# Gated attention, then a gated long convolution: the last batch's gate projections are put at the end of the planner's order, and the first loads are reordered

## The chip, the cores and the metric

The kernel runs on one core of one Trainium2 chip. Its time is the device time of the whole program in microseconds (us), the median of several runs. A profile of one execution shows what each engine did: PE is TensorE (PEld its weight loads), DVE is VectorE, ACT is ScalarE, POOL is GpSimd, SP is the engine that here only issues DMAs.

## The reference

For each of 8 batches, with u and v of 3136 x 256 and z of 3136 x 64:

```
attn = relu(z z^T / S)^2              # S = 3136
x    = u * (attn v)                   # 3136 x 256
x1, x2, x3 = split(x @ w_proj)        # three times 3136 x 256
conv = irfft(rfft(x2) * rfft(filter)) # circular convolution over the sequence
out  = (x1 * conv * x3) @ w_out
```

## The kernel before, in words

The sequence is cut into 25 tiles of 128 rows (the last holds 64) and into seven chunks of 512, 384, 512, 384, 512, 384 and 448 columns. For each batch and chunk the kernel makes score tiles (`score_mm`, L1334), takes their relu on ScalarE (L1509), squares them on ScalarE or VectorE (L1516, L1518) and multiplies them with v into two accumulators (`weigh`, L1364). Part of the squared tiles are turned by a transposing DMA and used again for a later chunk (L1449). The chunk's result times u is `xT` (L1558), the transposed x.

From `xT`, `add_proj` makes two things. `to_gates` computes x1 (L896), copies it out of PSUM, computes x3 (L908) and multiplies the two into a gate tile (L916), for each half of the 256 columns: 14 gates a batch. `to_spectrum` computes x2 (L939), puts it through the first stage of a Fourier transform (L756) and writes it to DRAM. When all seven chunks of a batch are written, `add_spectrum` loads them in another order (L788), does the second stage (L809, L817), multiplies with the filter's spectrum (L1011), goes back (L809, L825) and writes to DRAM again (L1061). `add_end` loads that (L800), does the last stage (L1100, L1097), multiplies with the gates into `yT` (L1103), multiplies with w_out (L1131) and stores the output (L1159).

None of this is issued in the order of the code. The steps are tasks of a planner (`Plan`), which runs when the kernel is built: it keeps a model of each engine's time, takes for each engine the task that can start first, and so writes out each engine's instruction order, which the chip then follows strictly. For TensorE there are five queues: S (scores), W (attention times v), FA (projections and first transform stage), FB (spectrum and outputs) and FZ. In each of the last three the first six tasks are looked at, in S and W only the first one. A queue comes into play when its task can start now; FZ is always the last of the list:

```
order += ["FA", "FB", "W", "FZ"] if self.credit > 0 else ["W", "FA", "FB", "FZ"]
```

For the other engines a task's `prio` decides among those that can start at the same time; a lower number goes first. A `Pool` of n buffers is in the planner a row of n slots: a task that takes a slot waits until an earlier one is free. `ps_m` is the pool of two PSUM banks through which projections, spectrum and outputs go; once no W task is left, the planner also lends them the other banks.

Around the end: the gates are FA tasks. Batch 6 stores three of its seven output chunks during batch 7 (FB); the other four are FZ tasks that wait for the last square of batch 7, and their stores wait until the last spectrum load of batch 7 is issued. The seven output chunks of batch 7 are FB tasks, with buffers borrowed from pools that are no longer used. An output chunk's last transform stage waits for all 14 gates of its batch.

At the start, before the planner: ten DMAs load z of batch 0 (L451), seven issued by SP and three by ScalarE; POOL issues the loads of v and u (L418, L399) in the order v tiles 0 to 6, u chunk 0, v tiles 7 to 13, u chunk 1, w_proj (L473), v tiles 14 to 24. `V_AT` and `U_AT` are the times at which the planner takes v (first part, rest) and u (chunk 0, chunk 1) as there. The table `T1` of the first transform stage is a sine (L636) of angles that VectorE makes.

## Time and profile before

| | us |
|---|---|
| median of 3 runs (lowest, highest) | 1051.87 (1051.53, 1052.62) |
| the profiled execution, whole | 1055.78 |
| its span, first to last instruction | 1053.9 |

| engine | busy us | share of the span | instructions |
|---|---|---|---|
| PE | 1003.5 | 95% | 6078 |
| DVE | 819.7 | 78% | 1485 |
| ACT | 914.6 | 87% | 1285 |
| POOL | 185.2 | 18% | 401 |

The mean granted clock of TensorE is 0.981 of full speed. The DMAs moved 167.99 MB, 159 GB/s over the span. Matmuls are pipelined and their ends are modelled, so 95% for PE is not 95% of its peak. A busy share over the whole span mixes stages with different limits: the start, eight batches, and a tail after the last attention matmul. The chain of work that ended last is followed back from the last instruction, at each step to what released it.

### The profile page before, as it was taken

The page shows a single profiled execution, that of the slowest core. Times are in us where ns is not written, and L with a number is a line of the kernel's source. Part 1 is how long each engine was busy: PE and PEld are TensorE (multiplying, and loading weights), DVE is VectorE, ACT ScalarE, POOL GpSimd, SP SyncE. Part 2 cuts the span into 40 slices and gives each one's busy share as a digit, 9 for nine tenths or more (in the row PEclk, how much of TensorE's full clock was granted, in tenths as well). Part 3 has the DMA queues.
Part 4 walks back from the last instruction along what each step waited for, and adds up shares of the span by engine and source line. Part 5 has one row for each costly group of instructions (what it writes and reads, how often), then busy time and mean ns, then how long its engine had stood idle before and what let it go on. Part 6 is the DMA issues. An engine that isn't in the chain of part 4 may idle for free.

```text
span 1053.9 us, 17942 instructions
## 1 busy us (share of the span) xinstructions
PE 1003.5 (95%) x6078; PEld 487.5 (46%) x6078; DVE 819.7 (78%) x1485; ACT 914.6 (87%) x1285; POOL 185.2 (18%) x401
## 2 busy tenths in 40 slices
PE   5999899999999999999999999999999999999874
PEld 2443434444444444445444454445454454444553
DVE  6767479968798688887889777986889877997653
ACT  6998799979899699998899899997999989997642
POOL 5123111211022201222022210212021210010000
PEclk9999999999999999999999999999999999999966
DMA  9699857888878878898979888888888888666447
GB/s 155 108 165 176 157 114 140 158 153 191 174 152 132 160 178 183 162 150 185 183 134 170 158 192 188 148 151 145 185 177 167 157 170 188 127 133 151 109 149 203
DMA packets 324380, 167.99 MB, mean 159 GB/s; under 512 B 234088, under 2 KB 302184, under 8 KB 324288
## 3 DMA queue, kind: packets, MB, share of 16 engines
q1 hardware_dynamic: 296320, 135.69, 60.0%
q0 software_dynamic: 27728, 30.97, 21.4%
q8 instruction: 48, 0.79, 0.3%
q14 instruction: 44, 0.36, 0.1%
q10 hardware_dynamic: 240, 0.18, 0.1%
HBM read 90.26 MB, written 53.35 MB: 136 GB/s over the span
## 4 chain that ended last, share of the span: by engine, by line
PE 75%; DVE 7%; DMA 7%; ACT 6%; issue 3%; SPq 2%; ACTq 0%; DVEq 0%; POOL 0%; POOLq 0%
PE ps_o_t L1364 38%; PE ps_s_t L1334 11%; PE ps_m_t L908 4%; PE ps_m_t L939 4%; PE ps_m_t L896 3%; PE ps_m_t L1131 3%; ACT R_t L1509 3%; PE ps_m_t L756 2%; DMA M_t<-A_t 2%; DVE xT_t L1558 2%; PE ps_m_t L817 2%; DVE A_t L1518 2%; PE ps_m_t L1100 2%; PE ps_m_t L825 2%; DVE xh L1011 2%
## 5 line engine op out<-in xcount | busy, mean ns | idle before, releaser
L1509 ACT ACTIVATE R_t<-ps_s_t 128x1024 f32<-128x1024 f32 (+2 forms) x552 | 485.6, 917 | 30.4 <-PE ps_s_t L1334 23.2
L1364 PE MATMUL ps_o_t<-A_t,v_t 128*128 128x512 bf16 (+2 forms) x2064 | 471.1, 354 | 1.8 <-DVE A_t L1518 1.5
L1364 PEld LDWEIGHTS <-v_t 128*128 128x128 bf16 x2688 | 253.0, 98 | 239.7 <-issue 33.4
L1518 DVE TENSOR_TENSOR A_t<-R_t 128x1024 bf16<-128x1024 f32 (+3 forms) x286 | 305.5, 1075 | 44.0 <-ACT R_t L1509 33.0
L1516 ACT ACTIVATE A_t<-R_t 128x1024 bf16<-128x1024 f32 (+4 forms) x266 | 251.2, 953 | 11.9 <-DMA M2e_t<-A_t 3.0
L1334 PE MATMUL ps_s_t<-zT_t 64*128 64x512 bf16 (+2 forms) x1088 | 155.1, 357 | 3.4 <-ACT R_t L1509 2.7
L408 POOL COPY tick<-xT_t 1x1 bf16<-1x1 bf16 x54 | 10.1, 188 | 748.4 <-DVE xT_t L1558 748.4
L916 DVE TENSOR_TENSOR gate_t<-ps_m_t,x_t 128x256 bf16<-128x256 f32 (+1 forms) x222 | 72.8, 382 | 40.5 <-PE ps_m_t L908 28.8
L1558 DVE SCALAR_TENSOR_TENSOR xT_t<-ps_o_t,uT_t 128x256 bf16<-128x256 f32 (+1 forms) x224 | 76.2, 381 | 30.8 <-PE ps_o_t L1364 17.0
L359 ACT ACTIVATE x_t<-ps_m_t 128x512 bf16<-128x512 f32 (+3 forms) x131 | 70.0, 557 | 25.1 <-PE ps_m_t L896 15.6
L1011 DVE TENSOR_TENSOR xh<-xh,H 100x1024 bf16<-100x1024 bf16 x120 | 81.6, 683 | 6.2 <-ACT xh L359 5.3
L1334 PEld LDWEIGHTS <-zT_t 64*128 64x128 bf16 x1088 | 33.2, 94 | 101.6 <-issue 97.8
L1364 PE MATMUL ps_o_t<-M_t,v_t 128*128 128x384 bf16 (+2 forms) x336 | 79.1, 345 | 1.1 <-DMA M_t<-A_t 1.1
L1103 DVE TENSOR_TENSOR yT_t<-ps_m_t,gate_t 128x512 bf16<-128x512 f32 (+2 forms) x98 | 59.3, 621 | 22.3 <-PE ps_m_t L1100 18.6
L363 DVE CAST x_t<-ps_m_t 128x512 bf16<-128x512 f32 (+3 forms) x90 | 54.9, 625 | 14.1 <-PE ps_m_t L939 8.0
L399 POOL DMA_DIRECT2D un_t<-in_u_dram x112 | 60.0, 558 | 6.9 <-issue 5.5
L418 POOL DMA_DIRECT2D v_t<-in_v_dram x112 | 59.7, 555 | 5.4 <-issue 2.4
L896 PE MATMUL ps_m_t<-xT_t,wp 128*128 128x512 bf16 (+2 forms) x222 | 56.1, 353 | 3.5 <-DVE xT_t L1558 3.0
L939 PE MATMUL ps_m_t<-wp,xT_t 128*128 128x256 bf16 x392 | 57.3, 274 | 0.0
L908 PE MATMUL ps_m_t<-xT_t,wp 128*128 128x512 bf16 (+2 forms) x222 | 54.8, 354 | 0.3 <-ACT x_t L359 0.2
L363 DVE CAST s_t<-ps_m_t 128x512 bf16<-128x512 f32 (+1 forms) x67 | 42.3, 640 | 15.0 <-PE ps_m_t L756 14.4
L359 ACT ACTIVATE xh<-ps_m_t 100x512 bf16<-100x512 f32 (+1 forms) x89 | 52.5, 612 | 0.6 <-PE ps_m_t L1131 0.4
(179 smaller groups left out, 965.5 us busy)
## 6 DMA issues: line engine op xcount, KB each, us to landing
out_dram<-ost_t SPq DMA_DIRECT2D x49, 256.0 KB
spec<-s_t SPq DMA_DIRECT2D x88, 128.0 KB
spec_in_t<-spec SPq DMA_DIRECT2D x28, 392.0 KB
spec<-gs_t SPq DMA_DIRECT2D x28, 392.0 KB
out_dram<-ost_t SPq DMA_DIRECT2D x47, 192.0 KB
v_t<-in_v_dram POOLq DMA_DIRECT2D x56, 128.0 KB, 4.3
un_t<-in_u_dram POOLq DMA_DIRECT2D x56, 128.0 KB, 5.1
conv_in_t<-spec SPq DMA_DIRECT2D x26, 256.0 KB
```

The costliest lines, as they stand in the source:

```text
L359: nc.scalar.activation(out_, in_, AF.Copy)
L363: nc.vector.tensor_copy(out_, in_)
L896: nc.tensor.matmul(box["p"][:, :cw], wp16[:, k, ds(nb * P, P)], xt["t"][:, k, :cw], start=(k == 0), stop=(k == 1),)
L908: nc.tensor.matmul(box["p3"][:, :cw], wp16[:, k, ds((4 + nb) * P, P)], xt["t"][:, k, :cw], start=(k == 0), stop=(k == 1),)
L939: nc.tensor.matmul(box["p"][:, ds(k_ * D, D)], xt["t"][:, k, ds((at + k_) * P, P)], wp16[:, k, ds(D, D)], start=(k == 0), stop=(k == 1),)
L1011: nc.vector.tensor_tensor(x[:, 1 - i], x[:, 0], h, ALU.mult)
L1334: nc.tensor.matmul(ps[:m, i, :cw], zt[h, ds(t * P, m)], zt[h, ds(C0[c], cw)], start=True, stop=True)
L1364: nc.tensor.matmul(o, row(v16[b], t)[:, ds(dh * P, P)], x, start=(k == 0 and i == 0), stop=(last and i == len(pair) - 1),)
L1509: nc.scalar.activation(box["R"][:rows, 0:n, :cw], live[un][:rows, 0:n, :cw], AF.Relu)
L1516: nc.scalar.activation(a, r, AF.Square)
L1518: nc.vector.tensor_tensor(a, r, r, ALU.mult)
L1558: nc.vector.scalar_tensor_tensor(x, f, inv_s2, ut, ALU.mult, ALU.mult)
```

## The change

The gate tasks of the last batch go to FZ instead of FA, and their two evictions get prio 2 instead of 0. The pool of x buffers has eight instead of two. An output chunk waits for its own gate alone, not for all of the batch. At the start SP issues all ten loads of z, and POOL issues v whole, then u chunks 0 and 1, then w_proj. The planner's times for v and u are set anew, and it takes the sine's first step as possible from 6.6 us.

```diff
-    xT_p = Pool("xT", 2, [P, 2, 512], BF16)
+    xT_p = Pool("xT", 8, [P, 2, 512], BF16)
...
-            q = nc.scalar if j == 0 and t0 == ZF else nc.sync
-            q.dma_start(
+            nc.sync.dma_start(
                 out=zf[lo // ZF][...], in_=zr[...]
             )
...
     load_rows(v16[0], v[0], 0, 7)
     u_nat = {}
-    cast_u(0, 0)
...
     load_rows(v16[0], v[0], 7, 14)
+    load_rows(v16[0], v[0], 14, NT)
+    cast_u(0, 0)
     cast_u(0, 1)
     wp16 = const.tile([P, 2, 3 * D], BF16, name="wp16")
     nc.gpsimd.dma_start(out=wp16[:], in_=moe_w_proj.rearrange("(t p) n -> p t n", p=P))
-    load_rows(v16[0], v[0], 14, NT)
...
-    ZF_AT, V_AT, U_AT = (4.5, 6.0, 7.0), (9.0, 16.0), (13.0, 18.0)
+    ZF_AT, V_AT, U_AT = (4.5, 6.0, 7.0), (8.0, 15.0), (19.0, 22.0)
...
-    def sin_steps(box, w, first, dst=None):
+    def sin_steps(box, w, first, dst=None, at=0.0):
...
-        ta = step("DVE", a, c_dve(w), takes=[gs_p.slots])
+        ta = step("DVE", a, c_dve(w), takes=[gs_p.slots], at=at)
...
-    t1_done, _ = sin_steps({}, P, t1_first, T1[:, :])
+    t1_done, _ = sin_steps({}, P, t1_first, T1[:, :], 6.6)
...
+        kind, late = ("FZ", 2) if b == B - 1 else ("FA", 0)
...
-                a = pe("FA", mm1, c_pe(cw, cw), xt_tasks, [ps_m.slots, x1_p.slots])
-                e1 = job(None, ev1, both(cw), [a])
+                a = pe(kind, mm1, c_pe(cw, cw), xt_tasks, [ps_m.slots, x1_p.slots])
+                e1 = job(None, ev1, both(cw), [a], prio=late)
                 e1.frees.append((a, 0))
-                a3 = pe("FA", mm3, c_pe(cw, cw), [*xt_tasks, a], [ps_m.slots, g_p.slots])
-                e3 = on("DVE", ev3, c_dve(cw), [a3, e1])
+                a3 = pe(kind, mm3, c_pe(cw, cw), [*xt_tasks, a], [ps_m.slots, g_p.slots])
+                e3 = on("DVE", ev3, c_dve(cw), [a3, e1], prio=late)
...
                 a = pe(
-                    kind, mm, c_pe(*[P] * nt), [ld, t4_done, *firsts, *(e for _, e in gtasks), *then],
+                    kind, mm, c_pe(*[P] * nt), [ld, t4_done, *firsts, gtasks[2 * c + dh][1], *then],
```

## The prediction

> **What bounds the kernel now.** I read four things in this order: the page's chain that ended last, the chain in order of time over the last batch, the busy table by stage, and the order of time at the head. One profiled execution took 1055.78 us with a span of 1053.9 us, so 1.9 us lie around the span; the median of the three runs is 1051.87, which is 3.9 lower. I sum against the profiled execution and carry the difference over to the median unchanged.

> The page's shares by engine:

> ```profile
> PE 75%; DVE 7%; DMA 7%; ACT 6%; issue 3%; SPq 2%; ACTq 0%; DVEq 0%; POOL 0%; POOLq 0%
> ```

> The same chain from 886.4 us to the last attention matmul of the last batch (batch 7) at 989.64, start and length of a piece in us; the gate projections are L896 and L908:

> ```profile
> 893.04 1.00 PE ps_m_t L896 x4
> 894.04 0.33 PE ps_o_t L1364 x2
> 894.36 0.43 PE ps_s_t L1334 x4
> 894.79 0.16 PE ps_o_t L1471 x2
> 894.96 0.97 PE ps_m_t L908 x4
> 895.93 0.97 PE ps_o_t L1364 x6
> ...
> 976.35 0.65 PE ps_m_t L896 x4
> ```

> One piece begins where the one before ends: TensorE is fed without a gap, so a matmul that leaves this stretch shortens it by its own length. The busy table by stage (length; busy us of PE, PEld, DVE, ACT, POOL; granted clock; DMA share; GB/s):

> ```profile
> 886.40:989.64 103.24, 102.95 (x622) 49.59 (x622) 83.41 (x151) 89.45 (x128) 6.92 (x16) 1.00 0.65 142
> 989.64:998.27 8.63, 6.93 (x68) 4.96 (x64) 7.30 (x16) 4.95 (x10) 0.00 (x0) 1.00 0.47 132
> 998.27:1026.00 27.73, 21.99 (x95) 15.68 (x95) 14.64 (x23) 15.16 (x27) 0.00 (x0) 0.63 0.47 142
> 1026.00:1031.50 5.50, 0.00 (x0) 0.00 (x0) 0.69 (x2) 0.00 (x0) 0.00 (x0) 0.71 0.76 199
> 1031.50:1053.90 22.40, 12.88 (x100) 9.80 (x100) 8.33 (x14) 7.10 (x15) 0.00 (x0) 0.65 0.74 198
> ```

> The first row is bound by TensorE at full clock. The others are the tail, a chain of latencies: last x, spectrum out and in (8.63 us), spectrum products (27.73), second round trip (5.50, every engine idle), output. There TensorE has gaps, but its clock falls to 0.63 to 0.71.

> **Gates out of the last batch.** On the chain between 886.4 and 989.64, L908 has 5.0% and L896 4.6%: 9.6% of 103.24 us = 9.9 us. This is chunks 0 to 5, 12 gates of four matmuls each (0.22 us for 512 columns); chunk 6 comes after the attention already. If all of them leave, TensorE loses 9.9 us here. VectorE loses about 24 products of 0.42 and 0.35 us (L916), 9 us, and 12 evictions of about 0.56 us, 6.7 us, leave ScalarE or VectorE. Do these two engines follow? From 900 to 940 they are busy 76.4 of 80 us; without two chunks' gates (four, 5.2 us) it is 71.2 of 2 x 36.6, or 97%. That is too tight to be free, so I give back 1.0 us there (between 0, if TensorE stays the bound, and 3, if the two become it). Gates that the planner drops into a hole of its own schedule stay in this stretch; they cost at most what they cost now. Main stage: **-8.9 us**.

> **The same gates in the tail.** They stand first in FZ, and the planner looks at six tasks of it, so they come ahead of batch 6's last four output chunks, which share that queue and now fill 989.64 to 998.27 (8 of their products L1103 and 20 matmuls L1131). A gate takes two PSUM banks and one of two x1 buffers; its chain of four operations takes about 2 us, so two in flight give one per 1.0 us, and VectorE alone allows one per 0.76. In 8.63 us 8 to 11 of the 14 gates get done; about 4.5 gates and nearly all of batch 6's end move on into the stage from 998.27. That is 4.5 x 0.83 = 3.7 us of matmul and 26 x 0.055 + 28 x 0.108 = 4.5, less 0.9 that lies there already: 7.3 us at full clock. VectorE and ScalarE get about 14 us more and have 13.1 + 12.6 idle, so they hide it. TensorE has 27.73 - 21.99 = 5.7 us idle. At the clock of 0.5 that the two-microsecond rows show from 1002 to 1014, 7.3 becomes 14.6, and the stage grows by 8.9. The 5.5 us round trip, where all is idle, takes some of that; with it the growth is 3.4. At full clock the stage needs 21.99 x 0.63 = 13.9 + 7.3 = 21.2 us of TensorE and (14.64 + 15.16 + 14) / 2 = 22 us of the other two, so it would shrink by 3 to 5. Which? The clock falls where TensorE goes slack:

> ```profile
> 996.00:998.00 2.00, 0.72 (x5) 0.41 (x5) 1.12 (x3) 0.87 (x2) 0.00 (x0) 1.00 0.58 189
> 998.00:1000.00 2.00, 1.29 (x7) 0.87 (x8) 0.00 (x0) 1.06 (x3) 0.00 (x0) 1.00 0.03 11
> 1000.00:1002.00 2.00, 0.74 (x4) 0.45 (x4) 1.91 (x3) 1.00 (x3) 0.00 (x0) 0.74 0.63 200
> 1002.00:1004.00 2.00, 2.00 (x11) 1.91 (x10) 0.77 (x2) 0.60 (x1) 0.00 (x0) 0.50 0.00 1
> ```

> The moved gates fill just these gaps, so I expect the fall later than now but not gone: **+2.0 us**, between -5 and +9. [...]

> Batch 6's stores (1728 rows of 1 KB, 1.77 MB) wait for the last spectrum load to be issued (1015.1 now), so a later end of batch 6 costs nothing until its products come after that. The stores then run at 230 to 320 GB/s, 6 to 8 us of DMA time. I take no cost, 0 to 7 as bounds.

> **Eight x buffers.** With two, x of chunk c+2 waits for the users of c; chunks lie about 16 us apart and the users end within that, so in batches 0 to 6 nothing waits on it, and the cost is nothing (only PE ps_m_t L896 <- DVE xT_t, 0.3 us, shows on PE between 868 and 989). In batch 7 they are the cover of the move: with two, deferred gates would stop x itself. The narrower wait of the outputs for their own gate changes nothing before batch 7, as the spectrum ends after the gates.

> **The head.** ScalarE's queue at the start, from order of time:

> ```profile
> 4.78 3.77 ACTq L451 DMA_DIRECT2D ost_t<-in_z_dram  x3
> 8.60 0.31 ACT L636 ACTIVATE T<-gs_t 128x128 bf16<-128x128 f32 x1 [6.35 <-DVE percol L607]
> 8.81 0.70 ACT L359 ACTIVATE xT_t<-ost_t 128x256 bf16<-128x256 f32 x2
> ```

> Its three z loads hold ScalarE until 8.55; the sine's input was ready at 7.1, so without them it can start up to 1.5 us earlier. ScalarE is then busy 23.5 of 24 us to 35 us, so an earlier start is carried on. SP gets three more issues of 0.60, ending near 7.0 instead of 5.2, before the two spectrum-padding writes; its next job is at 10.6, so that is hidden. On POOL the rest of v (7 issues, 4.2 us, with 1.0 us of waits on v's own landing) goes ahead of u: the issue of u moves from 3.7 and 7.9 to about 13, w_proj from 10.3 to about 15. With some 6 us to land, u is there near 20 and its transposes on SP, with the mirror transposes queued behind them, shortly after; x of chunk 0 is made at 33.7, so 10 us cover it. The DMAs are full (0.9 and more) from 3 to 26 us in either order. The head gives -1.5 to 0 by itself, but a planner's order changes with it, and batch 0 has stalls (88.6 to 96.4 on a mirror transpose, 117.5 to 125.2 on the filter's load) that may shift either way: **-1.0**, bounds -4 and +3.

> Sum: -8.9 + 2.0 - 1.0 = **-7.9 us**; profiled 1047.9, median **1044.0**.

> **Rivals.** (a) The gates keep the clock up through the spectrum: the stage falls from 27.7 to 22 and no gap re-opens, -6 instead of +2, and the median is 1036. For it: the gaps in the four rows above are what precedes the fall. Against: the stage's products still make TensorE wait 1 to 2 us each.
> (b) Slower: batch 6's end is pushed past the second round trip. Place: its products and output matmuls (9 us at half clock) stand among batch 7's outputs after 1031.5, and its 1.77 MB are stored with the final 3.2 MB, where DMA is at 0.74 already (6 to 8 us). It decides once fewer than about half of the 14 gates are through by 998 and the clock is at 0.5. Price: 9 of the spectrum stage's growth, 7 for stores; -8.9 - 1.0 + 16 = +6, with part of it overlapping +2 to +5: 1054 to 1057. For it: the queue's order. Against: the idle 5.5 us and the idle shares of DVE and ACT.
> (c) The change does not do what it says: the planner finds enough holes in its own schedule of batch 7, and the gates stay between the attention matmuls. Then only the head is left: about 1051, 1049 to 1053. Against: the chain shows no holes there.

> **Numbers.** Forecast 0.54 (1038 to 1049), (a) 0.13, (b) 0.22, (c) 0.11. A measurement of this kernel tells 0.2% (2.1 us) from no change. Only (c) reaches the middle, and it splits into 0.03 faster, 0.04 same and 0.04 slower: faster 0.54 + 0.13 + 0.03 = 0.70, same 0.04, slower 0.22 + 0.04 = 0.26. The range leaves out half of (a) and the upper part of (b): 1036 to 1055.

> **What would show it.** Right: between the last batch's start and its last attention matmul L896 and L908 fall from 9.6% of the chain to under 2%, and that matmul lies 9 to 11 us earlier; after it the two lines fill TensorE, and batch 6's L1103 come later than 998 does now by the new clock. The tail, 64.3 us from that matmul to the end of the span, becomes 61 to 70 us, with the granted clock at 1.0 some microseconds longer. At the head the sine starts near 7 and the first score matmul (10.87) up to 1.5 us earlier. Wrong: the last matmul earlier by under 6 us (ScalarE and VectorE bind), the tail longer by over 9 us, or a gap on TensorE before 60 us that waits for u or v.

## The result, and the profile after

The changed kernel takes 1044.33 us (1042.60 to 1045.57, four runs) where before took 1051.70 beside it: a ratio of 0.9927, interval 0.9910 to 0.9945, so 7.4 us faster (5.8 to 9.5). A second measurement, beside the experiments, gave 1043.34 against 1051.87, ratio 0.9906 (0.9884 to 0.9928). Single runs of either kernel lie up to 5 us from their median, and the first profile of before was of such a run (1055.78); the profiled run of the change took 1042.60, below its median. The two profiles are therefore 13.2 us apart where the medians are 7.4 apart, and the stages must be compared one by one.

The chain's shares, from the page of the changed kernel, are nearly the same as before:

```profile
PE 75%; DVE 8%; ACT 7%; DMA 5%; issue 3%; SPq 1%; another core or an unknown queue 0%; ACTq 0%; DVEq 0%; POOL 0%; POOLq 0%
```

The chain in order of time in the middle of the last batch (start, length in us). The gate lines are now L897 and L909, and attention, scores and spectrum follow one another without them:

```profile
930.24 0.97 PE ps_o_t L1365 x6
931.21 0.48 PE ps_s_t L1335 x4
931.70 0.32 PE ps_m_t L755
932.02 0.22 PE ps_m_t L824
932.24 1.30 PE ps_o_t L1365 x8
...
967.88 0.22 PE ps_m_t L909
...
968.15 0.59 PE ps_m_t L897 x2
```

Only one gate (its halves near 924 and 968) and the first half of another (968) were still run there. From 875 us on, the two gate lines have 0.81 us of the chain, under 1% where they had 9.6%. The other ten gates of chunks 0 to 5, and the rest of that one, come right after the last attention matmul, which ends at 979.42 instead of 989.64. In order of time on TensorE:

```profile
982.38 0.59 PE L897 MATMUL ps_s_t<-xT_t,wp 128*128 128x512 bf16 x2
982.82 0.59 PE L909 MATMUL ps_o_t<-xT_t,wp 128*128 128x512 bf16 x2
983.25 0.59 PE L897 MATMUL ps_o_t<-xT_t,wp 128*128 128x512 bf16 x2
983.68 0.59 PE L909 MATMUL ps_m_t<-xT_t,wp 128*128 128x512 bf16 x2
```

The busy table by stage, cut at the same events as before (length; busy us and instructions of PE, PEld, DVE, ACT, POOL; granted clock; DMA share; GB/s):

```profile
870.60:979.42 108.82, 107.90 (x653) 51.69 (x660) 82.79 (x139) 100.52 (x139) 7.45 (x19) 1.00 0.72 154
979.42:989.24 9.82, 9.30 (x55) 4.99 (x54) 8.18 (x24) 6.90 (x13) 0.00 (x0) 1.00 0.23 69
989.24:1014.06 24.82, 20.57 (x148) 14.30 (x148) 20.13 (x37) 17.74 (x34) 0.00 (x0) 0.98 0.50 152
1014.06:1019.63 5.57, 0.00 (x1) 0.00 (x1) 0.00 (x0) 0.65 (x2) 0.00 (x0) 0.50 0.88 241
1019.63:1040.70 21.07, 10.71 (x100) 8.41 (x100) 8.28 (x14) 6.99 (x15) 0.00 (x0) 0.82 0.72 208
```

(The first row here begins at the last x of batch 6; before's began at 886.4.) The stage of the spectrum products has 53 more matmuls than before and is 2.9 us shorter, and the clock stands at 0.98 where it was 0.63; whether the clock is the cause is tested below with matmuls that nothing reads. The two-microsecond rows that answer to the slack of before:

```profile
987.00:989.00 2.00, 1.77 (x13) 0.87 (x11) 1.89 (x7) 1.53 (x3) 0.00 (x0) 1.00 0.55 177
989.00:991.00 2.00, 1.76 (x11) 1.22 (x12) 1.57 (x5) 1.09 (x2) 0.00 (x0) 1.00 0.07 28
991.00:993.00 2.00, 1.90 (x18) 1.13 (x17) 2.00 (x4) 1.14 (x3) 0.00 (x0) 1.00 0.51 146
993.00:995.00 2.00, 1.34 (x8) 0.79 (x7) 2.00 (x6) 0.60 (x1) 0.00 (x0) 1.00 0.15 54
```

Where TensorE had 0.72, 1.29 and 0.74 of 2 us it now has 1.3 or more, and the clock stays at 1.00. VectorE becomes the full engine (2.00 of 2 us from 991 to 995).

Beside the page, one table serves all runs below. I cut each profile at the last product of x (chunk 6) of each batch; "tail" runs from that of batch 7 to the end of the span. Clock is the mean granted clock of the span. "Fill" stands for the matmuls of the left-out gates with nothing that reads them.

| kernel | batches 0-2 | 3-6 | 7 | tail | clock |
|---|---|---|---|---|---|
| before, first profile | 383.3 | 487.9 | 119.1 | 63.5 | 0.981 |
| before, second | 389.7 | 487.5 | 119.1 | 63.4 | 0.981 |
| the change, first | 381.5 | 489.1 | 109.6 | 60.6 | 0.992 |
| the change, second | 379.4 | 488.3 | 109.5 | 61.8 | 0.990 |
| tail's part alone | 383.2 | 487.2 | 111.0 | 63.8 | 0.988 |
| head's part alone | 379.9 | 489.1 | 120.0 | 63.4 | 0.984 |
| all but the gates' move | 382.4 | 488.8 | 120.4 | 62.7 | 0.984 |
| x buffers alone | 389.7 | 487.1 | 119.1 | 65.4 | 0.975 |
| before, no gates | 381.9 | 486.9 | 109.7 | 63.6 | 0.983 |
| before, no gates, fill | 383.6 | 487.2 | 110.6 | 61.5 | 0.990 |
| the change, no gates | 380.4 | 488.8 | 109.0 | 64.3 | 0.983 |
| the change, no gates, fill | 382.8 | 488.8 | 109.6 | 61.9 | 0.988 |
| the change, HOLD 2 | 379.2 | 488.7 | 107.8 | 60.9 | 0.992 |
| the change, half the gates | 383.0 | 489.6 | 115.3 | 64.2 | 0.985 |

The first column differs by 6 us between two executions of one program, so the comparisons rest on the third and fourth columns, on the timed runs, and on the first two columns only where several profiles agree. Two of the profiles are of runs far above the median of their kernel: that of the x buffers alone (1063.66 us, 6.3 above) and the second one of before (1061.44, 8.1 above).

The tail holds two effects that the table adds up. From the first spectrum product to the last matmul ahead of the second round trip, the fourteen profiles take 29.8 us at a granted clock of 0.50 (x buffers alone), 27.5 to 28.3 at 0.63 or 0.64 (six: both of before, the head's part, all but the gates' move, and the two without gates and without fill), 26.8 at 0.75 (half the gates) and 22.7 to 26.1 at 0.91 to 1.00 (the other six). From the last x to the first spectrum product they take 7.8 to 8.0 us where all gates of batch 7 stay in FA, and 8.5 to 10.7 in all others, 9.3 and 10.2 in the two that leave gates out and put nothing in their place. So a higher clock goes with a shorter spectrum stage; the longer way ahead of it, which the kernels without gates have too, takes a part of that back.

### The profile page after: what moved, and what is told of

Read it like the earlier page. It is cut to its first block, busy times and chain, and to the rows that moved or that the text cites. A ratio compares the mean times of both kernels' runs of the same rounds, so it can differ in the third digit from the quotient of the medians.

```text
span 1040.7 us, 17903 instructions
## 1 busy us (share of the span) xinstructions
PE 989.8 (95%) x6010; PEld 480.7 (46%) x6078; DVE 819.1 (79%) x1497; ACT 912.6 (88%) x1273; POOL 190.4 (18%) x401
## 4 chain that ended last, share of the span: by engine, by line
PE 75%; DVE 8%; ACT 7%; DMA 5%; issue 3%; SPq 1%; another core or an unknown queue 0%; ACTq 0%; DVEq 0%; POOL 0%; POOLq 0%
PE ps_o_t L1365 40%; PE ps_s_t L1335 11%; PE ps_m_t L940 4%; ACT R_t L1510 4%; PE ps_m_t L1132 4%; PE ps_m_t L909 3%; PE ps_m_t L897 3%; PE ps_m_t L755 2%; DMA M_t<-A_t 2%; PE ps_m_t L824 2%; PE ps_m_t L1101 2%; PE ps_m_t L816 2%; DVE xT_t L1559 2%; DVE A_t L1519 2%; ACT A_t L1517 1%
## 5 line engine op out<-in xcount | busy, mean ns | idle before, releaser
L1365 PE MATMUL ps_o_t<-A_t,v_t 128*128 128x512 bf16 (+2 forms) x2011 | 465.4, 354 | 3.6 <-issue 0.5
L1519 DVE TENSOR_TENSOR A_t<-R_t 128x768 bf16<-128x768 f32 (+2 forms) x271 | 290.7, 1080 | 35.2 <-ACT R_t L1510 29.4
L1517 ACT ACTIVATE A_t<-R_t 128x768 bf16<-128x768 f32 (+3 forms) x281 | 265.8, 958 | 5.4 <-DMA spec<-s_t 0.9
L408 POOL COPY tick<-xT_t 1x1 bf16<-1x1 bf16 x54 | 15.9, 294 | 737.5 <-DVE xT_t L1559 737.5
L917 DVE TENSOR_TENSOR gate_t<-ps_m_t,x_t 128x256 bf16<-128x256 f32 (+1 forms) x208 | 69.0, 385 | 30.8 <-PE ps_m_t L909 15.1
L359 ACT ACTIVATE x_t<-ps_m_t 128x512 bf16<-128x512 f32 (+3 forms) x114 | 61.7, 564 | 16.7 <-PE ps_m_t L897 12.2
L363 DVE CAST x_t<-ps_m_t 128x512 bf16<-128x512 f32 (+3 forms) x99 | 60.0, 621 | 15.6 <-PE ps_m_t L940 10.8
L1132 PE MATMUL ps_m_t<-wo,yT_t 128*128 128x256 bf16 (+1 forms) x348 | 54.9, 278 | 0.2
L897 PE MATMUL ps_m_t<-xT_t,wp 128*128 128x512 bf16 (+2 forms) x203 | 51.7, 353 | 2.0 <-DVE xT_t L1559 1.7
L1365 PE MATMUL ps_o_t<-M2e_t,v_t 128*128 128x512 bf16 (+1 forms) x192 | 51.7, 370 | 0.3 <-issue 0.2
```

Source lines behind the costliest of these rows:

```text
L363: nc.vector.tensor_copy(out_, in_)
L897: nc.tensor.matmul(box["p"][:, :cw], wp16[:, k, ds(nb * P, P)], xt["t"][:, k, :cw], start=(k == 0), stop=(k == 1),)
L917: nc.vector.tensor_tensor(g[:, ::-1] if h == 0 else g, p, x, ALU.mult)
L1132: nc.tensor.matmul(box["p"][:rows, ds(i * D, D)], yb["y"][:, k, ds((i0 + i) * P, rows)], wo16[:, k, :], start=(k == 0), stop=(k == 1),)
L1365: nc.tensor.matmul(o, row(v16[b], t)[:, ds(dh * P, P)], x, start=(k == 0 and i == 0), stop=(last and i == len(pair) - 1),)
L1517: nc.scalar.activation(a, r, AF.Square)
```

## The experiments

My theory: the gates leave a stretch that TensorE bounds and fit into the tail at a small cost, and the head gives a microsecond. The rivals: the clock in the tail pays for the move; or the gain lies in the first batches.

### The tail's part alone

```diff
 # before, with only these parts of the change
+    xT_p = Pool("xT", 8, [P, 2, 512], BF16)
+        kind, late = ("FZ", 2) if b == B - 1 else ("FA", 0)
+                    kind, mm, ..., [ld, t4_done, *firsts, gtasks[2 * c + dh][1], *then],
```

> The tail's part of the change alone (gates of batch 7 in FZ with prio 2, eight x buffers, the narrower wait), with the head as before. Forecast's terms: -8.9 us in the last batch and +2.0 in the tail, so -6.9 us against before, 1044.8. Clock theory (the moved gates keep TensorE's clock up and the tail itself gets shorter by 3 to 6 us): -12 to -15 us, and the time lost again at the head. Head theory (the gain comes from the first 60 us or from a new order of batches 0 to 6): 0 to -2 us.

Measured: 1046.73 us against 1051.87, ratio 0.9943 (0.9924 to 0.9961), 6.0 us faster (4.1 to 8.0). The forecast's -6.9 lies inside. But the profile spreads it otherwise: the last batch gives 8.1 us, and the tail is 63.8 us, neither the +2.0 of the forecast nor the -3 to -6 of the clock theory. Its spectrum stage did get shorter (26.1 us at a clock of 0.91, against 27.6 at 0.63), but the first spectrum product came 10.0 us after the last x instead of 7.9.

### The head's part alone

```diff
 # the change, with these three taken back
-    xT_p = Pool("xT", 8, [P, 2, 512], BF16)
+    xT_p = Pool("xT", 2, [P, 2, 512], BF16)
-        kind, late = ("FZ", 2) if b == B - 1 else ("FA", 0)
+        kind, late = "FA", 0
-..., gtasks[2 * c + dh][1], *then],
+..., *(e for _, e in gtasks), *then],
```

> The head's part alone (z by SP, v whole ahead of u, the planner's times for them), with gates, x buffers and waits as before. Forecast's term: -1.0 us, bounds -4 to +3. Clock theory: +4 to +7 us, since the tail's gain must then be lost here. Head theory: -5 to -7 us.

Measured: 1054.51 us, ratio 1.0027 (1.0010 to 1.0043), 2.8 us slower (1.0 to 4.5). The sign of the forecast is wrong, though its bounds (-4 to +3) hold the value, and the head theory falls. The two parts add up to -3.2 where the whole has -7.4 to -9.9. The table places most of this behind batch 6: the last batch and the tail together take 174.8 us with the tail's part alone, and 170.2 and 171.3 with the whole change. The clock does not tell the two apart: it stays at 1.00 for 31.4 us after the last x here, for 32.8 and 30.8 us there. The planner wrote two different orders; which step of them makes the difference is open.

### Before without the gates of chunks 0 to 5

```diff
+        if b == B - 1 and c < NC - 1:
+            ...   # no projections; the outputs of batch 7 read the gate tiles of batch 6
+            to_spectrum()
```

> Before, with the gate projections of batch 7 for chunks 0 to 5 left out (its outputs take batch 6's gates instead), so the 9.9 us of matmul leave the last batch and come back nowhere. Forecast's terms: -8.9 us against before, and faster than the tail's part alone by the +2.0 that the gates cost in the tail; the clock falls near the first spectrum product as in before. Clock theory: slower than the tail's part alone although it does less, by 3 to 6 us, since nothing fills the gaps ahead of the spectrum. If the last batch were bound by ScalarE and VectorE: -5 to -7 us.

Measured: 1044.39 us, ratio 0.9923 (0.9907 to 0.9940), 8.1 us faster. The forecast's -8.9 is inside, and with 9.4 us the last batch bears it out. The kernel is 2.3 us faster than the tail's part alone, where the clock theory had it 3 to 6 us slower. That is the +2 that I forecast for the gates in the tail, but the tail's own length does not show it (63.6 without, 63.8 with them); the two lie 1.3 us apart in the last batch. The pair differs in the x buffers too (two here, eight there), so it does not decide between the theories.

### The change once more

> The changed kernel once more, for a second profile of it on the chip on which the parts run. All theories: -7.4 us against before (interval -9.5 to -5.8). Forecast: the two parts of the change add up to it within 1.5 us. If the planner's new order in batches 0 to 6 matters, they do not add up.

Measured: ratio 0.9906 (0.9884 to 0.9928). The sizes of the stages repeat: 109.5 and 61.8 us. Beside the same before the whole has -9.9 us and the parts -3.2, so they miss each other by 6.7 us where I forecast at most 1.5.

### The matmuls without anything behind them

```diff
 # before without the gates, eight x buffers, and in their place
+            for w0 in (0, 1, 4, 5):
+                def fill(w0=w0): ...      # two matmuls into a bank that nothing reads
+                a = pe("FZ", fill, c_pe(cw, cw), xt_tasks, [ps_m.slots])
```

> As the kernel without gate projections in chunks 0 to 5 of batch 7 (outputs take batch 6's gates), but their 48 matmuls are kept as FZ tasks with nothing behind them (no eviction, no product; eight x buffers, narrower wait). If the granted clock is what pays for the moved work: clock 1.0 through the first 25 us of the tail, the tail (last x to the end of the span, 63.6 us without the gates, 63.5 before) down to 58 to 61 us, and the time 2 to 4 us below the kernel without gates, although it does 9.9 us more of matmul. If the moved work only lies in idle time and the clock is a bystander: tail 63 to 65 us and the time as without the gates, or slower.

Measured: 1046.47 us against 1053.30, ratio 0.9943 (0.9928 to 0.9958). The clock went up (a mean of 0.990, against 0.983 in the kernel without gates) and the tail down to 61.5 us, nearly to the 58 to 61 of the clock theory, but the time was 2 us above that of the kernel without gates, not below it. This kernel also has the eight buffers, which the other lacks, so the times cannot decide; the pair was therefore run again on the changed kernel, below.

### All but the gates' move, and the buffers alone

```diff
 # the change with
+        kind, late = "FA", 0
 # and, in the other kernel, before with
+    xT_p = Pool("xT", 8, [P, 2, 512], BF16)
+..., gtasks[2 * c + dh][1], *then],
```

> The changed kernel with the gates of batch 7 back in FA at prio 0: head, eight x buffers and narrower wait alone. If the buffers change the head (z's casts take x slots, and with two they wait for their transposes): -3 to -4 us against before, which is what the whole change has beyond the tail's part. If the buffers matter only in batch 7: +2 to +3, as the head alone. Forecast as written: -1.

> Before with eight x buffers and the narrower wait alone. Forecast: 0 (within 1 us). If the buffers speed up the start in any order of the loads: -2 to -4 us.

Measured: 1056.11 against 1053.30, ratio 1.0036 (1.0017 to 1.0056), and 1057.37, ratio 1.0048 (1.0030 to 1.0066). So neither head nor buffers help without the move: +3.8 and +5.0 us, and no theory had foreseen a loss from the buffers. The step from "all but the gates" to the whole change is then -11.5 us (from 1.0036 to 0.9927) to -13.7 us (to 0.9906), more than the 9.9 us of matmul that were moved. The table accounts for it: 10.8 and 10.9 us in the last batch, 2.1 and 0.9 in the tail. What shortens the tail is left to explain.

### Before once more

> Before once more, for a second profile: its first profile was of an execution some 4 us above the median. All theories: last batch 119 us and tail 63.5 us again, as the other kernels with these parts show; the 4 us lie in batches 0 to 6.

Measured in one run: 1061.44 us, with 119.1 us in the last batch and 63.4 in the tail. This run's span is 5.7 us longer than that of the first profile, and its batches 0 to 2 are 6.4 us longer, so the difference lies there.

### The change without those gates, and with their matmuls alone

The same two edits as above, made on the changed kernel, so that head, buffers and the planner's times are equal in the pair.

> The changed kernel with the gate projections of batch 7's chunks 0 to 5 left out (its outputs take batch 6's gates), so head, buffers and planner's times are those of the change. If the moved gates pay for themselves through the clock: last batch 109.5 us as in the changed kernel, clock down to 0.5 to 0.7 from the spectrum on, tail 63 to 64 us against 60.6 and 61.8, and the time equal to the changed kernel's or up to 3 us slower. If, as forecast, they cost 2.0 us in the tail: 2 us faster than the changed kernel.

> The kernel of g1_after_no_gates with the 48 left-out matmuls kept as FZ tasks that nothing reads. Clock theory: clock 1.0 for the first 25 us of the tail, tail 59 to 61.5 us, 2 to 4 us faster than g1_after_no_gates although it does 9.9 us more of matmul. Bystander theory: as g1_after_no_gates or slower.

Measured on one chip: 1045.80 us without the gates, ratio 0.9932 (0.9912 to 0.9953), and 1043.68 us with the unread matmuls, ratio 0.9911 (0.9886 to 0.9936). The medians are 2.1 us apart in the direction of the clock theory, though the intervals overlap. The clocks do not overlap: 0.978 to 0.983 in every run without, 0.986 to 0.991 in every run with them. The tail by ten microseconds from the last x, without the gates:

```profile
978.15:988.15 10.00, 6.64 (x59) 4.74 (x59) 6.68 (x14) 4.84 (x10) 0.00 (x0) 0.97 0.23 68
988.15:998.15 10.00, 8.67 (x31) 6.20 (x32) 4.56 (x7) 4.59 (x9) 0.00 (x0) 0.52 0.26 76
998.15:1008.15 10.00, 6.99 (x37) 4.87 (x37) 6.66 (x11) 5.20 (x10) 0.00 (x0) 0.82 0.49 153
```

and with them as unread matmuls:

```profile
981.20:991.20 10.00, 10.00 (x63) 5.67 (x61) 0.40 (x2) 3.26 (x6) 0.00 (x0) 1.00 0.23 69
991.20:1001.20 10.00, 8.99 (x82) 7.20 (x80) 10.00 (x21) 7.15 (x16) 0.00 (x0) 1.00 0.32 98
1001.20:1011.20 10.00, 7.37 (x50) 5.06 (x48) 7.72 (x13) 7.89 (x15) 0.00 (x0) 1.00 0.77 226
```

In the first ten microseconds TensorE is busy 10.00 instead of 6.64, mostly with the unread matmuls. In the second ten the clock is 1.00 instead of 0.52, and it gets through 82 matmuls instead of 31; 46 of the 82 are of batch 6's output steps, most of which ran earlier in the other kernel, and 36 against 31 are of the spectrum. The tail is 2.4 us shorter (61.9 against 64.3) although 42 of the 48 unread matmuls, 8.3 us of TensorE, were added to it. The spectrum stage alone is 4.8 us shorter (22.7 against 27.5), and the second round trip takes 1.7 us of it back (7.8 against 6.1). Nothing reads these matmuls, so they can help only by keeping TensorE busy or by the order that the planner writes around them; the spectrum's matmuls of 512 columns, which in before follow each other after 0.22 us at a clock of 1.00 and after 0.43 at 0.50, speak for the first. The real gates give the tail the same length (60.6 and 61.8). So in the changed kernel the moved gates cost nothing in the tail: the kernel that leaves them out is not faster.

### Half of the gates

```diff
-        kind, late = ("FZ", 2) if b == B - 1 else ("FA", 0)
+        kind, late = ("FZ", 2) if b == B - 1 and c > 2 else ("FA", 0)
```

> The changed kernel with only the gates of chunks 3 to 6 of batch 7 in FZ, so 4.7 us instead of 9.9 leave the last batch. If each moved gate brings its own matmul time and the clock follows the fill: +5 to +6 us against the changed kernel, tail 61 to 63.5. If the gain came mostly from the clock and a little fill is enough: +3 or less. If it came from elsewhere: 0.

Measured: 1052.98 us against 1052.47, ratio 0.9997 (0.9981 to 1.0014): some 8 to 9 us behind the change, more than the +5 to +6 of any theory. Of these the last batch has 5.7 us (115.3 against 109.6) and the tail 2.4 to 3.6 (64.2 against 60.6 and 61.8). Half the fill keeps the clock up for 19 us after the last x, against 33 and 31 in the change:

```profile
987.94:997.94 10.00, 9.38 (x80) 6.24 (x79) 8.13 (x22) 7.02 (x14) 0.00 (x0) 1.00 0.24 69
997.94:1007.94 10.00, 5.59 (x40) 4.02 (x38) 8.52 (x14) 4.91 (x10) 0.00 (x0) 0.97 0.36 108
1007.94:1017.94 10.00, 9.02 (x37) 6.99 (x36) 4.07 (x7) 5.83 (x11) 0.00 (x0) 0.52 0.57 179
```

The clock falls at 1007.30, after this stretch in which TensorE was busy 1.28 of 3.41 us:

```profile
1003.89:1007.30 3.41, 1.28 (x7) 0.53 (x5) 3.41 (x7) 1.60 (x3) 0.00 (x0) 1.00 0.51 142
```

The spectrum stage is then 26.8 us, between the two groups, and the tail is a little longer than before's. Half of the gates are not enough; how many are was not measured.

### One output chunk more in the tail

```diff
-HOLD = 3
+HOLD = 2
```

> The changed kernel with HOLD 2 instead of 3: one more output chunk of batch 6 (8 matmuls of 128 columns, 16 of 256, 2.2 us, two products, two evictions) goes from the last batch to the tail. If the tail still has room: -2 us against the changed kernel. If VectorE and TensorE are full there now (9.7 and 8.9 of 10 us): 0 to +3 us.

Measured: 1040.24 us against 1052.47, ratio 0.9884 (0.9861 to 0.9907), the fastest kernel of all: 12.2 us faster than before, about 3 us faster than the change by the medians (its interval overlaps with that of the change's second measurement). The last batch loses 1.7 to 1.8 us more (107.8), and the tail stays at 60.9, so it still had room.

## Why the prediction was right

The time came out at 1044.33 where 1044.0 was forecast. Term by term it is less good: one was nearly right, and two missed in opposite directions, so that the total came so close is luck.

- **The last batch, -8.9 us.** Measured 9.5 and 9.6 us in the two profiles of the change (119.1 to 109.6 and 109.5), and 10.4 to 10.9 against the kernels with the same head (120.0, 120.4). The give-back of 1.0 us for ScalarE and VectorE was hardly needed: with the same head and without any of these gates the batch takes 109.0, so the gates that stayed cost at most about 0.5 us there. The last attention matmul came 10.2 us earlier (989.64 to 979.42), within the 9 to 11 forecast; 0.7 us of that lies ahead of the last batch.
- **The gates in the tail, +2.0 us.** Measured -1.7 and -2.9. This is the mis-sized term: I took the clock as falling somewhat later, and it did not fall until 1012.9, 33 us after the last x instead of 11. Of the two ends that I worked out, 3 to 5 us less at full clock and up to 9 more at half, the first was right, and the row to trust was the one that showed what precedes the fall. The working at full clock (21.2 us of TensorE, 22 us for the other two engines) met 20.57 us of TensorE, and (20.13 + 17.74) / 2 = 18.9 us for the others, in a stage of 24.82: the work was sized well, but no engine fills the stage, so its length is not that of the busiest. Only two gates instead of 4.5 were left for it, and all of batch 6's output matmuls. Two things lessen the gain: the path from the last attention matmul to the first spectrum product became longer (9.82 instead of 8.63), as in the kernels without the gates, and VectorE is full from 991 to 1005 (1.97 or 2.00 of every 2 us). Rival (a) had the mechanism but not the price: the stage fell by 2.9 us, not to 22.
- **The clock.** Before's clock is 1.00 or 0.50 and changes near 1001.0, 1014.6, 1018.0, 1024.8 and 1028.3; the pieces between these are 13.65, 3.41, 6.83 and 3.41 us long, close to four, one, two and one times 3.41. In the 3.41 us ahead of the first fall TensorE was not idle but busy 1.43 us:

```profile
997.54:1000.95 3.41, 1.43 (x8) 0.87 (x8) 0.86 (x2) 2.04 (x5) 0.00 (x0) 1.00 0.29 90
```

  (The three two-microsecond rows ahead of the 0.50 in the prediction hold 3.25 us without a matmul.) What I worked out for half clock, where the moved 7.3 us of matmul take 14.6, did not happen: with the moved gates the spectrum stage ran at a clock of 0.98 where before's ran at 0.63. With half of them the clock stayed up only until 9.3 us after the first spectrum product.
- **The head, -1.0 us.** Measured alone +2.8 (1.0 to 4.5), with the buffers +3.8 (1.8 to 5.9). The steps that I named went differently. ScalarE was free early, and the first score matmul came at 6.48 instead of 10.87, but then ScalarE waited for the next part of z:

```profile
4.88 0.42 ACT L359 ACTIVATE xT_t<-ost_t 128x256 bf16<-128x256 f32 x1 [2.63 <-DMA ost_t<-in_z_dram]
9.25 0.83 ACT L359 ACTIVATE xT_t<-ost_t 128x320 bf16<-128x320 f32 x2 [3.96 <-DMA ost_t<-in_z_dram]
...
17.84 0.32 ACT L635 ACTIVATE T<-gs_t 128x128 bf16<-128x128 f32 x1
```

  The sine, forecast near 7, came at 17.84, and the first chunk's x ended at 36.5 instead of 36.0. What an earlier ScalarE gained was given back to a DMA. No gap of TensorE before 60 us waits for u or v, as forecast. Yet the head does gain behind that: batch 0 ends at 130.7 to 131.9 us in all eight profiles with the new head, and at 135.5 to 140.8 in all six with the old one. Batch 1 gives a part of this back (125.0 to 129.6 us, against 123.4 to 126.4); why is open. Then the planner's other order costs time far from the head: in all eight profiles with the new head batches 3 to 6 take 488.3 to 489.6 us, in all six with the old one 486.9 to 487.9, and batch 7 with its gates in place takes 120.0 and 120.4 instead of 119.1. Of the difference in batches 3 to 6, batch 4 has 1.4 us (123.2 or 123.3 in all eight, 121.8 in all six). That is about 2 us of the loss. What batches 0 to 2 gain or lose together cannot be told from profiles that differ by 6 us between executions.
- **Eight x buffers, nothing.** Alone, with the narrower wait, they cost 5.0 us (3.2 to 7.0). Where is open: its one profile, of a run 6.3 us above the median, has a long batch 0 (140.8 us) and a tail in which the clock stays at half for 41 us (65.4 us), but the tail's part alone has the same buffers and the old head, and its batch 0 takes 137.6. Their slots are also what z's casts take at the start, so the planner's order can change from there on. That batch 7 needs them as a cover for the move was not tested: no run moves the gates with two buffers.
- **Rivals (b) and (c).** Batch 6's end did come later: its eight products end in the stage from 989.24. But all were done before the second round trip, and its stores were issued from 1005.9 to 1015.9, and the other condition of (b), too few gates through and the clock at half by the first spectrum product, was not met: the matmuls of 12 of the 14 gates were through and the clock was at 1.00. So its price was not paid. (c) did not happen.

Sum with measured terms: -9.5 - 2.3 (the mean of -1.7 and -2.9) + 2.8 to 3.8 = -9.0 to -8.0, between the two measurements of -7.4 and -9.9. About 1 us of the head's cost lies in batch 7 with its gates in place (120.0 and 120.4 against 119.1) and is counted twice in this; without it the sum is -9.9 to -9.3. The forecast's total was right since a tail that was 4.3 us better and a head that was about 4 us worse than I sized them cancel. What the move gains in the last batch is shown by the kernels without the gates. That the tail gets shorter with the clock rests on the stages and clocks of the pair with and without fill; its times alone (2.1 us apart, intervals that overlap) would not decide it. Why the head and the buffers cost what they cost is open.

## What to carry to other kernels

Work of lowest priority that is moved from a stage bound by TensorE into a tail of latencies can pay twice: by its own length (here 9.5 us), and by keeping TensorE busy enough to hold its clock for the work that is on the path (here 0.98 instead of 0.63 in the spectrum stage, and 1.7 to 2.9 us of tail). It takes enough of it (half the gates left the tail at 64.2 us), so look in the two-microsecond rows for what precedes each fall of the clock and ask whether the moved work covers that. With a planner that writes the order, a local edit at the start also changes the order of everything behind it, so its cost is to be measured alone before it is kept.

## What the runs showed of the hardware that I had not expected

Two executions of one program differ by up to 6 us in the first three batches (383.3 and 389.7 us), while batches 3 to 6 repeat within 1 us and the last within 0.1.
